# Row maxima stored by a transfer of single floats instead of through a transpose, and more places for visits of seven row maxima beside the mlp

## The chip, the cores and the metric

The kernel runs on one core of one Trainium2 chip, in one launch. The metric is the time of one execution on the device in microseconds (us). Five engines work side by side, each through its own list of instructions: PE (matrix products; PEld is its loading of the stationary operand), DVE (vector work and reductions), ACT (activations and copies), POOL (elementwise work, and it issues some transfers), and SP, which only issues transfers. They wait for one another through semaphores.

## What is computed

The reference, cut to what matters (S = 2048 tokens, D = 448, H = 16 heads of 28, F = 1792):

```python
g = sigmoid((x * gate_w).sum(-1, keepdims=True))
q, k, v = split_heads(x @ wqkv)                    # 16 heads of 28
scores = einsum("bhqd,bhkd->bhqk", q, k) * 28 ** -0.5
a = merge_heads(softmax(scores) @ v) @ wo
h = gelu(layernorm(x) @ w1 + b1)                   # 2048 x 1792
b = h @ w2 + b2
return g * a + (1 - g) * b
```

The softmax needs, for every head and every query, the largest score of its row. The kernel computes these row maxima in a pass of their own, ahead of the scores that are exponentiated.

## The kernel before, in words

**Stages.** Until 113 us PE computes q, k and v. From 113 us to 457 us the mlp runs in four column chunks `c` of 512 tokens: `mlp1` (L626: 14 tiles of 11 products each, into bank 0 or 7 by turns) and `mlp2` (L644: 4 tiles of 42 products each, also into banks 0 and 7 by turns). From 457 us to the end the attention runs over 16 chunks `n = 4 g + c`: four groups of four heads, four chunks of 512 queries.

PSUM is used as eight banks of 128 x 512 floats, `bank[:, 0]` to `bank[:, 7]`.

**Row maxima.** `RowMax` (L387) makes them for chunk after chunk. One chunk is 64 products of 28 x 512 (4 heads `j`, 4 query tiles `i`, 4 key pieces `k`; L450), each into a bank, each followed by a reduction of that bank along its row on DVE (L431; neighbouring banks in one instruction). The 64 columns of results are reduced to 16 (L461, tile `mf`, 128 x 16: a query's number within its tile is the partition). Then the chunk has to be closed (`close`, L410): PE transposes `mf` with the identity into a bank (L412), DVE multiplies the 16 x 128 result by -1 (L415, tile `mt`), and a transfer writes it to DRAM (L416, `ms`), where each head's 512 maxima lie in a row. The closing takes a place among the products as a 65th one: in the last bank of the first call of `issue` after the chunk's 64th product. 16 chunks are so 16 x 65 = 1040 places. `load_qm` (L556) later reads four rows of `ms` into the 29th row of each head in `qh`, so that the score product of 29 rows subtracts the maximum by itself. For the last chunk, that transfer is issued from step 12 of the 16 steps of the attention chunk before.

**Where the maxima stand on PE.** The order on PE is written out by the program. Beside the mlp, `Filler.run` is called after each product of the mlp (after some of `mlp2`'s), counts slots, and starts a *visit* when enough maxima are due: six products into banks 1 to 6, or seven, when the caller allows it (`seven(i)`, L622): then the bank of the neighbouring tile, 0 or 7, is used first. Seven are allowed after the products 4 to 7, counted from 0, of a tile of `mlp1` (not in the first column chunk) and for `f` from 1 to 11 in `mlp2`. Where only six are allowed, a visit waits until eight are due (`wait` = 2). `clear` keeps a visit from coming before DVE has reduced the one before it. `MLP_MAX` places (488) are spread over the mlp.

In the attention, PE alternates between the scores of five units (a unit: one head, 128 keys, 512 queries, three products, L577; U = 5) and the products of probabilities with v (L865). I call one such round a *slot*. A slot holds up to three maxima (`scores`, L567: one into bank 5 ahead, one into bank 6 in the middle, one into bank 5 at the end). The rest of the 1040 places is spread over 186 slots. When all of them are done, the slots become *late* ones: seven units in two halves, of four and three or of three and four (UL = 7), with the products with v between the halves, and no maxima.

**Queues.** Beside the mlp, SP issues the stores of the maxima (L416) and the loads of `qd` (L403), among the loads of the layernorm's input (L130) and the stores of the mlp's output (L663). In the attention `self.queue` is POOL: it issues the stores L416 and the loads L403 between its elementwise work and the transfers of `finish` (L783, L787, L789).

Of the kernel before, what the change touches and what calls it, by code (L numbers as in the profile page):

```python
# [30 lines left out]
MLP_MAX = 488  # L31
# [12 lines left out]
def kernel(ctx: ExitStack, tc: tile.TileContext, xt, wqk, wv, wo, xk, w1, b1, w2, b2,  # L44
# [17 lines left out]
    ms = [dram.tile([4, S], F32, name=f"ms{g}") for g in range(NG)]  # L62
# [324 lines left out]
    class RowMax:  # L387


        def __init__(self):  # L390
            self.queue = nc.sync
            self.qds = {}
            self.done = 0
            self.last = None
            self.load(0)
            self.begin(0)
# [13 lines left out]
        def close(self, ps):  # L410
            g, c = divmod(self.n - 1, NC)
            nc.tensor.transpose(ps[:4 * TPC, :P], self.last, ident)  # L412
            self.last = None
            mt = mpool.tile([4 * TPC, P], F32R, name="mt")
            nc.vector.tensor_scalar(mt, ps[:4 * TPC, :P], -1.0, None, op0=OP.mult)  # L415
            self.queue.dma_start(ms[g][:, c * CH:(c + 1) * CH].rearrange("j (i x) -> j i x", x=P), mt.bitcast(F32))  # L416

        def issue(self, banks, rows=None, close=65):

            held, closing = [], self.last is not None
# [11 lines left out]
            for b in banks:  # L434
                left = sum(len(x) for x in self.left)
                closes = closing and b == banks[-1] and left <= close
                if not (left or closes):
                    break
                self.done += 1
                if closes:  # L440
                    reduce()
                    self.close(bank[:, b])
                    continue
# [14 lines left out]
                if left == 1:  # L458
                    reduce()
                    self.last = mpool.tile([P, 4 * TPC], F32, name="mf")  # L460
                    nc.vector.reduce_max(self.last.rearrange("p (j i) -> p j i", j=4),  # L461
                                         self.mx.rearrange("p (k i j) -> p j i k", k=4, j=4), axis=AX)
                    if self.n + 1 < NG * NC:
# [103 lines left out]
    def scores(units, most, tiles, between=None, opening=None):  # L567
# [19 lines left out]
        if most > 0:  # L587
            filler.max.issue([5], [(units[0] + 3) % 4], close=56)
# [8 lines left out]
        for i in range(3):  # L597
            for p in last:
                product(p, i)
            if i == 0 and most > 1:  # L600
                filler.max.issue([6], [(units[0] + 1) % 4, (units[0] + 2) % 4], close=-1)
# [398 lines left out]
```

## Time and profile before

| | |
|---|---|
| median of 3 runs | 1100.08 us (1099.73 to 1100.36) |
| the profiled execution, its own time | 1099.34 us |
| its span, first to last instruction | 1097.5 us |
| PE busy | 1090.4 us (99% of the span) |
| DVE busy | 737.1 us (67%) |
| ACT busy | 638.1 us (58%) |
| POOL busy | 334.2 us (30%) |
| PE's granted clock, mean | 0.999 |
| products of row maxima (L450) | 1024 |
| transposes of row maxima (L412) | 16, 4.4 us in all |

How to read the rows that follow: a timeline row gives the start in us from the beginning of the span, the time from the first to the last instruction of the row, the engine, the line of the program, the operation, what it writes and reads, the shape, and how many instructions were merged into the row. Products overlap, so the distance from one start to the next says more than the length of a row. A group row gives count, busy time and the mean of one instruction in ns, then the idle time ahead of them and what ended it. Rows of waits name who waited for whom, with the total, the number of times and the longest. Rows of one line give the shortest, median and longest duration in ns. In the slots of the attention each product with v appears as two products in the timeline.

### The profile page before, as it was taken

The page shows a single profiled execution, that of the slowest core. Times are in us where ns is not written, and L with a number is a line of the kernel's source. Part 1 is how long each engine was busy: PE and PEld are TensorE (multiplying, and loading weights), DVE is VectorE, ACT ScalarE, POOL GpSimd, SP SyncE. Part 2 cuts the span into 40 slices and gives each one's busy share as a digit, 9 for nine tenths or more (in the row PEclk, how much of TensorE's full clock was granted, in tenths as well). Part 3 has the DMA queues.
Part 4 walks back from the last instruction along what each step waited for, and adds up shares of the span by engine and source line. Part 5 has one row for each costly group of instructions (what it writes and reads, how often), then busy time and mean ns, then how long its engine had stood idle before and what let it go on. Part 6 is the DMA issues. An engine that isn't in the chain of part 4 may idle for free.

```text
span 1097.5 us, 19765 instructions
## 1 busy us (share of the span) xinstructions
PE 1090.4 (99%) x8150; PEld 667.4 (61%) x8150; DVE 737.1 (67%) x958; ACT 638.1 (58%) x658; POOL 334.2 (30%) x357
## 2 busy tenths in 40 slices
PE   9999999999999999999999999999999999999998
PEld 7888877777778777744444444444444444464545
DVE  4553598988888988566766766666666767746103
ACT  5434651331240231478878878878878878848572
POOL 5015565243334340013202320321223024343260
PEclk9999999999999999999999999999999999999999
DMA  7988531011121032262000220012111003002011
GB/s 268 355 273 289 174 112 65 9 47 51 40 52 46 18 80 72 69 153 61 28 19 19 65 73 19 20 29 53 36 51 37 19 20 95 13 26 70 35 53 59
DMA packets 53078, 84.34 MB, mean 77 GB/s; under 512 B 8516, under 2 KB 28500, under 8 KB 52076
## 3 DMA queue, kind: packets, MB, share of 16 engines
q1 hardware_dynamic: 48732, 76.27, 22.4%
q0 software_dynamic: 4256, 6.81, 2.5%
q8 instruction: 64, 1.05, 0.4%
q14 instruction: 26, 0.21, 0.1%
HBM read 56.40 MB, written 26.49 MB: 76 GB/s over the span
## 4 chain that ended last, share of the span: by engine, by line
PE 96%; DVE 1%; issue 1%; ACT 1%; DMA 0%; SPq 0%; DVEq 0%; ACTq 0%
PE bank L865 22%; PE bank L577 20%; PE bank L450 15%; PE bank L634 12%; PE bank L221 5%; PE bank L650 4%; PE bank L656 4%; PE bank L651 4%; PE bank L233 3%; PE bank L323 2%; PE bank L762 1%; PE bank L763 1%; PE bank L764 1%; DVE mx L431 1%; DMA raw<-in_xt 0%
## 5 line engine op out<-in xcount | busy, mean ns | idle before, releaser
L431 DVE TENSOR_REDUCE mx<-bank 128x1 f32<-128x512 f32 (+2 forms) x735 | 635.1, 897 | 197.4 <-PE bank L450 184.3
L581 ACT ACTIVATE pt<-bank 128x1536 f32<-128x1536 f32 (+1 forms) x387 | 461.6, 1243 | 119.0 <-PE bank L577 119.0
L865 PE MATMUL bank<-pt,vg 128*32 128x512 f32 x1948 | 260.4, 602 | 0.1
L450 PE MATMUL bank<-khi,qd 28*128 28x512 f32 x512 | 241.3, 479 | 0.5
L450 PEld LDWEIGHTS bank<-khi,qd 28*128 28x128 f32 x512 | 92.3, 181 | 146.2 <-DVE mx L431 108.1
L577 PE MATMUL bank<-qh,klo 28*128 28x512 f32 x1024 | 172.3, 391 | 0.0
L577 PE MATMUL bank<-qh,khi 29*128 29x512 f32 x768 | 155.5, 480 | 0.8 <-ACT khi L581 0.5
L634 PE MATMUL bank<-y,w1f 128*128 128x512 f32 x616 | 152.0, 397 | 0.0
L634 PEld LDWEIGHTS bank<-y,w1f 128*128 128x128 f32 x616 | 112.6, 188 | 33.0 <-issue 11.1
L577 PE MATMUL bank<-ql,khi 28*128 28x512 f32 x768 | 128.8, 391 | 0.0
L642 POOL TENSOR_TENSOR hl<-h,hh 128x512 fp32r<-128x512 f32 x56 | 73.0, 1303 | 117.4 <-ACT hh L641 92.4
L783 POOL DMA_DIRECT2D lt<-ob x15 | 10.8, 723 | 273.0 <-DVE ob L782 248.7
L640 ACT ACTIVATE h<-bank,b1s 128x512 f32<-128x512 f32 x56 | 38.6, 689 | 94.8 <-PE bank L634 94.7
L865 PEld LDWEIGHTS bank<-pt,vg 128*32 128x32 f32 x1948 | 44.6, 108 | 77.3 <-issue 73.1
L577 PEld LDWEIGHTS bank<-qh,klo 28*128 28x128 f32 x1024 | 86.1, 185 | 3.4
L577 PEld LDWEIGHTS bank<-qh,khi 29*128 29x128 f32 x768 | 60.3, 182 | 39.7 <-ACT pt L581 24.3
L650 PE MATMUL bank<-w2h,hh 128*128 128x448 f32 x224 | 83.7, 374 | 0.0
L656 PE MATMUL bank<-w2h,hl 128*128 128x448 f32 x224 | 83.2, 372 | 0.0
L651 PE MATMUL bank<-w2l,hh 128*128 128x448 f32 x224 | 81.2, 363 | 0.0
L662 ACT ACTIVATE h<-bank 128x448 f32<-128x448 f32 x16 | 8.7, 546 | 123.0 <-PE bank L656 67.7
L450 PE MATMUL bank<-khr,qd 28*128 28x512 f32 x512 | 72.6, 460 | 0.2 <-DVE mx L431 0.2
L577 PEld LDWEIGHTS bank<-ql,khi 28*128 28x128 f32 x768 | 64.9, 185 | 11.9
(142 smaller groups left out, 1220.5 us busy)
## 6 DMA issues: line engine op xcount, KB each, us to landing
qk<-hl SPq DMA_DIRECT2D x28, 512.0 KB
raw<-in_xt SPq DMA_DIRECT2D x16, 256.0 KB
vs<-vt SPq DMA_DIRECT2D x16, 256.0 KB
s<-in_xt SPq DMA_DIRECT2D x16, 256.0 KB
rc<-rls POOLq DMA_DIRECT2D x60, 64.0 KB, 2.3
w1f<-in_xk SPq DMA_DIRECT2D x8, 448.0 KB
gbs<-h SPq DMA_DIRECT2D x16, 224.0 KB
klo<-qk SPq DMA_DIRECT2D x16, 224.0 KB
```

The lines of the kernel that those rows point to most:

```text
L221: nc.tensor.matmul(ps, a, b, start=(i == 0), stop=(i == len(ops) - 1))
L431: nc.vector.reduce_max(self.mx[:, at:at + n], bank[:, b:b + n] if n > 1 else bank[:, b], axis=AX)
L450: nc.tensor.matmul(bank[:, b], self.qds[self.n][r, i * P:(i + 1) * P], khi[self.n // NC][r, k * 512:(k + 1) * 512], start=True, stop=True)
L577: nc.tensor.matmul(bank[:, p], a[r, k * P:(k + 1) * P], b[r], start=(i == 0), stop=(i == 2))
L581: nc.scalar.activation(t, bank[:, at[0]:at[-1] + 1], AF.Exp, scale=SCALE)
L634: nc.tensor.matmul(ps, a, b, start=(i == 0), stop=(i == len(ops) - 1))
L640: nc.scalar.activation(h, ps, AF.Gelu_apprx_tanh, bias=b1s[:, f:f + 1])
L642: nc.gpsimd.tensor_sub(hl[f], h, hh[f].bitcast(F32))
L650: nc.tensor.matmul(a, hh[f][:, sl], w2h[f], start=(f == 0), stop=False)
L651: nc.tensor.matmul(a, hh[f][:, sl], w2l[f], start=False, stop=False)
L656: nc.tensor.matmul(a, hl[f][:, sl], w2h[f], start=False, stop=(f == NF - 1))
L865: nc.tensor.matmul(pv[32 * j:32 * j + 32, :], vg[n // NC][:, k, 32 * j:32 * j + 32], probs.pop(4 * step + j), start=(k == 0), stop=(k == N ...
```

## The change

- `close` goes, and with it the 16 transposes on PE, the 16 multiplications of 16 x 128 out of PSUM on DVE, and 16 places: a chunk has 64 places, all of them 1024.
- Instead, right behind the reduction to `last` (128 x 16), DVE multiplies that tile by -1 (`neg`), and a transfer writes it to DRAM as it lies: 128 partitions of 16 floats, each float to its own place, because neighbouring floats of a partition belong 128 floats apart. The transfer always stands in SP's queue, in the attention too. Each chunk has a tensor `ms` of its own.
- `MLP_MAX` is 475 instead of 488. In the attention the remaining places are spread at three per slot.
- Visits of seven are allowed after the products 3 to 8 of a tile of `mlp1` (before 4 to 7) and for `f` from 1 to 12 in `mlp2` (before 1 to 11).

```diff
-MLP_MAX = 488
+MLP_MAX = 475
...
-    ms = [dram.tile([4, S], F32, name=f"ms{g}") for g in range(NG)]
+    ms = [dram.tile([4, CH], F32, name=f"ms{n}") for n in range(NG * NC)]
...
-        def close(self, ps):
-            g, c = divmod(self.n - 1, NC)
-            nc.tensor.transpose(ps[:4 * TPC, :P], self.last, ident)
-            self.last = None
-            mt = mpool.tile([4 * TPC, P], F32R, name="mt")
-            nc.vector.tensor_scalar(mt, ps[:4 * TPC, :P], -1.0, None, op0=OP.mult)
-            self.queue.dma_start(ms[g][:, c * CH:(c + 1) * CH].rearrange("j (i x) -> j i x", x=P), mt.bitcast(F32))
...
                 if left == 1:
                     reduce()
-                    self.last = mpool.tile([P, 4 * TPC], F32, name="mf")
-                    nc.vector.reduce_max(self.last.rearrange("p (j i) -> p j i", j=4),
+                    last = mpool.tile([P, 4 * TPC], F32, name="mf")
+                    nc.vector.reduce_max(last.rearrange("p (j i) -> p j i", j=4),
                                          self.mx.rearrange("p (k i j) -> p j i k", k=4, j=4), axis=AX)
+                    neg = mpool.tile([P, P], F32R, name="mt")[:, :4 * TPC]
+                    nc.vector.tensor_scalar(neg, last, -1.0, None, op0=OP.mult)
+                    nc.sync.dma_start(ms[self.n].rearrange("j (i p) -> p (j i)", p=P), neg.bitcast(F32))
...
-        while filler.done < min(65 * NG * NC, 65 * (n + 1) + 9):
+        while filler.done < 64 * (n + 1):
             filler.max.issue([5])
         g, c = divmod(n, NC)
-        nc.sync.dma_start(qs[n][0][DH:P:32].bitcast(F32), ms[g][:, c * CH:(c + 1) * CH])
+        nc.sync.dma_start(qs[n][0][DH:P:32].bitcast(F32), ms[n])
...
-                filler.run(W1, seven(f) if 4 <= i < 8 else (), 2)
+                filler.run(W1, seven(f) if 3 <= i < 9 else (), 2)
...
-            more = seven(i) if 0 < f < NF - 2 else ()
+            more = seven(i) if 0 < f < NF - 1 else ()
...
-    filler.spread(nc.gpsimd, NG * NC * 65, ((NG * NC - 2) * NT + LQ - 1) * 4 // U - 2)
+    filler.spread(nc.gpsimd, NG * NC * 64, -(-(NG * NC * 64 - filler.done) // 3))
```

What this does to the order of the instructions, in numbers counted over the whole of PE's list:

| | before | changed |
|---|---|---|
| visits beside the mlp | 74 | 71 |
| of seven places / of six | 38 / 36 | 47 / 24 |
| products of maxima beside the mlp | 475 | 473 |
| transposes beside the mlp / in the attention | 7 / 9 | 0 / 0 |
| products of maxima in the attention | 549 | 551 |
| slots with maxima or a transpose | 187 | 184 |

Of the visits, `mlp1` has four fewer and `mlp2` one more. A line number of the changed kernel is lower by 10 to 15 behind the deleted function: its L435 is L450 of before, L565 is L577, L622 is L634, L853 is L865, L549 is L561, and the store stands at L450.

PE, second tile of `mlp1` in the second column chunk, before (`w1f_900` is this tile's weights, `y` the layernorm's output, `khr` and `qd` the two operands of the maxima; `w1f_927` belongs to the next tile):

```order
L634 MATMUL bank<-y_100,w1f_900 128x512
L634 MATMUL bank<-y_101,w1f_900 128x512
L634 MATMUL bank<-y_100,w1f_900 128x512 x2
L450 MATMUL bank<-khr,qd 128x512 x6
L634 MATMUL bank<-y_101,w1f_900 128x512
L634 MATMUL bank<-y_100,w1f_900 128x512 x2
L634 MATMUL bank<-y_101,w1f_900 128x512
L634 MATMUL bank<-y_100,w1f_900 128x512 x3
L634 MATMUL bank<-y_100,w1f_927 128x512
```

The same tile in the changed kernel (its weights are `w1f_912`, the next tile's `w1f_939`):

```order
L622 MATMUL bank<-y_112,w1f_912 128x512
L622 MATMUL bank<-y_113,w1f_912 128x512
L622 MATMUL bank<-y_112,w1f_912 128x512 x2
L622 MATMUL bank<-y_113,w1f_912 128x512
L622 MATMUL bank<-y_112,w1f_912 128x512 x2
L622 MATMUL bank<-y_113,w1f_912 128x512
L622 MATMUL bank<-y_112,w1f_912 128x512
L435 MATMUL bank<-khr,qd 128x512 x7
L622 MATMUL bank<-y_112,w1f_912 128x512 x2
L622 MATMUL bank<-y_112,w1f_939 128x512
```

The visit of six after product 3 has become a visit of seven after product 8; two products follow it, then the next tile begins in the bank that the visit used first.

PE, end of the last slot with maxima and what follows, before (`khi` and `klo` are the keys, `pt` probabilities):

```order
L450 MATMUL bank<-khi_3882,qd 128x512
L577 MATMUL bank<-qh,klo 128x512 x2
L577 MATMUL bank<-ql,khi_3882 128x512 x2
L865 MATMUL bank<-pt_9734,vg 32x512
L865 MATMUL bank<-pt_9757,vg 32x512 x3
L412 MATMUL bank<-ident,mf 16x128
L577 MATMUL bank<-qh,khi_3882 128x512 x3
L577 MATMUL bank<-qh,klo 128x512 x3
L577 MATMUL bank<-ql,khi_3882 128x512 x3
```

The same place in the changed kernel, three slots earlier in the program:

```order
L435 MATMUL bank<-khi_3890,qd 128x512
L565 MATMUL bank<-qh,klo 128x512 x2
L565 MATMUL bank<-ql,khi_3890 128x512 x2
L435 MATMUL bank<-khi_3890,qd 128x512
L853 MATMUL bank<-pt_9674,vg 32x512
L853 MATMUL bank<-pt_9684,vg 32x512 x2
L853 MATMUL bank<-pt_9709,vg 32x512 x3
L853 MATMUL bank<-pt_9719,vg 32x512 x2
L565 MATMUL bank<-qh,khi_3890 128x512 x4
```

The slot of five units that began with the transpose is gone; the first late group, four units and then three, follows at once.

SP, around the load of the last chunk's maxima (`qh<-ms`), before; the store that it reads stood in POOL's queue:

```order
L852 DMA vg<-gbs 128x4x448
L770 DMA out_y<-klo 128x448
L561 DMA qh<-ms_74 4x512
L770 DMA out_y<-klo 128x448 x3
L852 DMA klo<-gbs 128x4x448
```

And in the changed kernel, where the store (`ms_86<-mt`) stands in the same queue, directly ahead of the load:

```order
L840 DMA vg<-gbs 128x4x448
L450 DMA ms_86<-mt 128x16x1
L549 DMA qh<-ms_86 4x512
L758 DMA out_y<-klo 128x448 x4
L840 DMA klo<-gbs 128x4x448
```

More of the change, by code (lines that the diff above doesn't have):

```diff
@@ L435, in issue @@
                 left = sum(len(x) for x in self.left)
-                closes = closing and b == banks[-1] and left <= close
-                if not (left or closes):
+                if not left:
                     break
                 self.done += 1
[L440 to L443, printed above, removed]
                 most = max(range(4), key=lambda j: (len(self.left[j]), -j))
@@ L587, in scores @@
         if most > 0:
-            filler.max.issue([5], [(units[0] + 3) % 4], close=56)
+            filler.max.issue([5], [(units[0] + 3) % 4])
         if opening:
@@ L878 @@
         while u < 4 * steps:
-            if not late and filler.done >= NG * NC * 65:
+            if not late and filler.done >= NG * NC * 64:
                 late = [(mpool.tile([P, S], F32, name="khr", bufs=1) if g == MLP_G else
```

9 lines of the change are left out of this document (4 added, 5 removed).

## Prediction

> **What bounds the kernel now.** I read the page's busy times first, then the chain that ended last, then a table of busy times by stage: the mlp, and the attention while it has maxima.
>
> ```profile
> PE 1090.4 (99%) x8150; PEld 667.4 (61%) x8150; DVE 737.1 (67%) x958; ACT 638.1 (58%) x658; POOL 334.2 (30%) x357
> PE 96%; DVE 1%; issue 1%; ACT 1%; DMA 0%; SPq 0%; DVEq 0%; ACTq 0%
> 113.50:456.90 343.40, 343.19 (x1788) 261.02 (x1787) 290.65 (x218) 103.57 (x165) 128.84 (x100) 1.00 0.21 59
> 456.90:1015.00 558.10, 557.52 (x5269) 266.19 (x5268) 380.17 (x613) 441.43 (x374) 139.39 (x189) 1.00 0.18 47
> ```
>
> The reader is to see that PE holds the end in both stages: busy for 343.19 of 343.40 us, and 557.52 of 558.10 us (columns: PE, PEld, DVE, ACT, POOL). So what counts is how long PE's list is, in time between starts. DVE is the nearest rival beside the mlp: 290.65 of 343.40 us, 85%.
>
> **Visits beside the mlp.** The timeline of PE in `mlp1` has visits of six, of seven and one with a transpose:
>
> ```profile
> 211.44 0.73 PE L450 MATMUL bank<-khr,qd 28*128 28x512 f32 x6
> 212.11 3.24 PE L634 MATMUL bank<-y,w1f 128*128 128x512 f32 x13
> 215.28 0.74 PE L450 MATMUL bank<-khr,qd 28*128 28x512 f32 x6
> ...
> 219.12 0.74 PE L450 MATMUL bank<-khr,qd 28*128 28x512 f32 x7
> 219.78 4.17 PE L634 MATMUL bank<-y,w1f 128*128 128x512 f32 x17
> 223.88 0.73 PE L450 MATMUL bank<-khr,qd 28*128 28x512 f32 x5
> 224.54 0.28 PE L412 MATMUL bank<-ident,mf 128*16 128x128 f32 x1
> 224.58 0.71 PE L634 MATMUL bank<-y,w1f 128*128 128x512 f32 x2
> ```
>
> From visit to visit it is 3.84 us with 13 products of the mlp and 4.76 us with 17: 0.92 / 4 = 0.23 us for a product, and 3.84 - 13 x 0.23 = 0.85 us for a visit of six. The visit of seven costs the same: 4.76 - 17 x 0.23 = 0.85. Until the mlp goes on, a six takes 0.67 us (211.44 to 212.11) and a seven 0.66. Four heads lie in four row groups and run together, so the seventh product finds room. The price hangs on the visit, and a seven carries one maximum more for nothing. `mlp2` has the same price:
>
> ```profile
> 442.80 0.36 PE L651 MATMUL bank<-w2l,hh 128*128 128x448 f32 x1
> 443.09 0.73 PE L450 MATMUL bank<-khr,qd 28*128 28x512 f32 x7
> 443.76 0.47 PE L656 MATMUL bank<-w2h,hl 128*128 128x448 f32 x1
> 444.07 0.37 PE L650 MATMUL bank<-w2h,hh 128*128 128x448 f32 x1
> 444.27 0.36 PE L651 MATMUL bank<-w2l,hh 128*128 128x448 f32 x1
> ```
>
> 442.80 to 444.07 holds two steps of 0.20 (444.07 to 444.27) and the visit: 1.27 - 0.40 = 0.87. The order has 74 visits before and 71 now: **-3 x 0.85 = -2.55 us**. A visit that ends in a transpose lasts 0.70 us (223.88 to 224.58) against 0.67: seven such, **-0.2 us**.
>
> **Slots of the attention.** Starts of the first maximum of slots in a row (that of 661 us is left out), then a slot with a transpose, then late slots of three and four units:
>
> ```profile
> 652.42 0.50 PE L450 MATMUL bank<-khi,qd 28*128 28x512 f32 x1
> 655.98 0.49 PE L450 MATMUL bank<-khi,qd 28*128 28x512 f32 x1
> 658.67 0.50 PE L450 MATMUL bank<-khi,qd 28*128 28x512 f32 x1
> ...
> 664.08 0.50 PE L450 MATMUL bank<-khi,qd 28*128 28x512 f32 x1
> ```
>
> ```profile
> 562.29 0.50 PE L450 MATMUL bank<-khi,qd 28*128 28x512 f32 x1
> 563.88 0.28 PE L412 MATMUL bank<-ident,mf 128*16 128x128 f32 x1
> 565.08 0.49 PE L450 MATMUL bank<-khi,qd 28*128 28x512 f32 x1
> ...
> 1052.37 0.50 PE L577 MATMUL bank<-qh,khi 29*128 29x512 f32 x3
> 1054.28 0.51 PE L577 MATMUL bank<-qh,khi 29*128 29x512 f32 x4
> 1056.18 0.50 PE L577 MATMUL bank<-qh,khi 29*128 29x512 f32 x3
> ```
>
> A slot is 2.70 us, every fourth, with two steps of v, 3.56 us: four take 664.08 - 652.42 = 11.66 us for 20 units, 0.583 us a unit. A late pair takes 1056.18 - 1052.37 = 3.81 us for seven units, 0.544 us. Three slots fewer move 15 units from one price to the other: 15 x (0.544 - 0.583) = **-0.6 us**. The slot with a transpose in the place of a maximum takes 2.79 us against 2.70: the 128-row transpose stops the row groups from running together. There are eight of them (the ninth is one of the three slots counted). Each costs between 0.09, as here, and 0.28, the transpose's own length, if nothing runs beside it; I take 0.13, nearer to the slot that is measured: **-1.1 us**.
>
> **What the change puts in.** On DVE, L415 goes and a multiplication of 128 x 16 comes, in the same instruction list directly behind L461. Its nearest row is a reciprocal of the same shape; the two rows of the maxima's reductions stand below it:
>
> ```profile
> L785 DVE RECIPROCAL lt<-lt x15: 242/244/254, 500.0 to 1046.7; 128x16 f32<-128x16 f32 x15
> L431 DVE TENSOR_REDUCE mx<-bank x546: 675/691/694, 460.1 to 1011.8; 128x1 f32<-128x512 f32 x182
>   PE bank L450: 140.0, 177
> ```
>
> At 0.24 us as L785 it delays the next reduction, and by that bank 5 for the next slot, in nine slots: at most 9 x 0.24 = 2.2 us; nothing where DVE waits for PE, as it does ahead of 177 of the 546 reductions in the attention (140.0 us, last row). I take **+0.4 us**, nearer to nothing because most of DVE's slack lies there.
>
> A visit of seven after product 8 of `mlp1` leaves two products until the next tile writes the bank that the visit used first. In this row DVE begins 0.53 us after the visit of 203.24:
>
> ```profile
> 203.24 0.74 PE L450 MATMUL bank<-khr,qd 28*128 28x512 f32 x7
> 203.77 2.89 DVE L431 TENSOR_REDUCE mx<-bank 128x1 f32<-128x512 f32 x2 [0.38 <-PE bank L450]
> ```
>
> With 0.69 for the bank (L431 above) it is free 1.22 us after the visit's start; the next tile arrives after 0.67 + 0.31 + 0.23 = 1.21 us (0.31 is the first step behind a visit, 443.76 to 444.07). So about 0.1 us for a semaphore; the order has two such visits: **+0.2 us**, up to 1.4 if DVE is a whole reduction, 0.69, late in both.
>
> The store: 16 times 2048 floats that are not neighbours in DRAM.
>
> ```profile
> L416 SPq DMA_DIRECT2D ms<-mt x7: 599/612/668, 186.4 to 433.8; - x7
> DMA to landing us min/median/max: 1.7/1.8/2.6
> L542 SPq DMA_DIRECT2D vg<-vs x8: 386/446/1045, 413.0 to 795.2; - x8
> q1 hardware_dynamic: 48732, 76.27, 22.4%
> ```
>
> Issuing costs SP no more than before: `vg<-vs` has 4 or 12 x 128 separate rows, 512 or 1536 pieces, and takes 0.45 us, against 0.61 us for the store's 16 pieces. The landing isn't shown by any row. Below, 1.8 us as L416. Above, a packet for each float at SP's mean: 0.224 x 16 x 1097.5 / 48732 = 0.081 us; over 16 engines 128 x 0.081 = 10.3 us. What hides it: nobody reads `ms` soon but for the last chunk. Behind the store in SP's queue are loads that are wanted a chunk later and the mlp's stores; SP stands waiting for other engines between them anyway. Cost 0, with either landing. POOL loses nine stores from its queue and nobody waits for POOL here.
>
> The Trainium skill, "DMA: Bandwidth & Descriptors", "Rules for kernel authors", speaks against this change: a last dimension with a stride becomes one descriptor per element, and a plain transfer that transposes is called 19 times slower than the hardware's transpose. No run here shows a transfer of single floats; 19 x 1.8 would be an estimate of 34 us for one store.
>
> **Sum.** -2.55 - 0.2 - 0.6 - 1.1 + 0.4 + 0.2 = -3.85 us, taken as -3.8. The profiled execution's own 1099.34 us (span 1097.5) becomes 1095.5; it lies 0.7 under the median 1100.08, from which I count: **1096.3 us**. With the bounds: 0.28 for each of the eight and no new wait give -2.55 - 0.2 - 0.6 - 2.2 = -5.6, 1094.5 us; 0.09 each, 2.2 on DVE and 1.4 in the mlp give -2.55 - 0.2 - 0.6 - 0.7 + 2.2 + 1.4 = -0.4, 1099.7 us. This kernel's measurement tells about 0.2% (2.2 us) from no change, so between 1097.9 and 1102.3 counts as none.
>
> **Rival 1: DVE paces the mlp.** 473 maxima need DVE as long as 475 did. If PE, three visits shorter, only comes earlier to banks not yet reduced, the 2.55 us go into waits and 1.25 remain: 1098.8 us. For it: DVE's 85%. Against it, the waits of PE's loads for a reduction in the window from 180 to 456 us (total, times, longest):
>
> ```profile
> PEld bank L450 <- DVE mx L431: 0.6, 2, 0.3
> ```
>
> PE's loads waited for DVE twice in all that time. Chance 0.14.
>
> **Rival 2, slower: the last store lands late and holds the last chunk.** Its place is the load `qh<-ms` of chunk 15, directly behind the store on SP. Before:
>
> ```profile
> 1012.57 0.27 DVE L461 TENSOR_REDUCE mf<-mx 128x16 f32<-128x64 f32 x1
> 1036.64 0.50 PE L577 MATMUL bank<-qh,khi 29*128 29x512 f32 x4
> ```
>
> The last reduction ended at 1012.84; chunk 15 starts at 1036.64, 23.8 us later. Now the maxima end ten units earlier in the program (unit 925 and not 935 follows), at 0.544 another 5.4 us: 29.2 us. Multiplication 0.24, issue 0.6, load 0.5 + 1.8 leave 26 us for the landing. At 10.3 us nothing happens. If the floats go over four engines only, by the four rows of `ms`, 512 x 0.081 = 41.5 us, and PE stands for 15.5 us: 1096.3 + 15.5 = 1111.8 us. It decides from a landing of 26 us, 0.2 us a float over 16 engines; it is slower by over 0.2% from about 32 us. Against it: the store's source has 128 partitions. Chance 0.07.
>
> The skill's 34 us would cost 8 us here; its rule on how many engines a transfer uses ("How many engines (k)", under "Why a DMA increments its semaphore by 16 and not by 1", same page) takes the slowest dimension of both sides, 128 here, and so sixteen engines. By that rule there is no stall; no run here shows the spread.
>
> **Rival 3: more comes back.** In the attention POOL held the store L416 among its elementwise work. One wait on DVE may come from that:
>
> ```profile
> DVE lt L785 <- DMA lt<-ob: 5.4, 3, 4.2
> ```
>
> The transfers `lt<-ob` stand in the same queue of POOL; DVE waited 5.4 us for them in three places, with reductions behind it. Without that, up to 1.5 us more (I let a good quarter reach PE): 1094.8 us. Chance 0.06.
>
> That the change doesn't do what it says is excluded by the order: 71 visits, no transposes.
>
> **Chances.** My forecast 0.73, of which 0.66 is faster by over 0.2% and 0.07 within it; rival 1 0.14, of which 0.03 and 0.11; rival 2 0.07, slower by 0.06 with 0.01 within; rival 3 0.06, faster. Faster 0.75, within 0.2% 0.19, slower 0.06. The range 1094.5 to 1099.5 takes in the forecast's bounds but for the last 0.2 us, and rivals 1 and 3, and leaves out rival 2.
>
> **What would show it.** Right: no L412; 71 visits, still 0.85 us; the mlp's end near 454 us and not 457; slots at a chunk's end within 0.1 us of 2.70; stores landing within 26 us. Wrong: waits of PE's loads for L431 beside the mlp well over 0.6 us (rival 1), slots behind L449 over 2.9 us (the multiplication's term), PE idle ahead of chunk 15 (rival 2), or SP's `qd` or layernorm loads late enough to hold PE (none of my terms).

## The result and the profile after

The changed kernel takes **1148.56 us** (median of 5 runs, 1147.51 to 1151.35) against 1100.08 us before: ratio 1.0447, 95% interval 1.0431 to 1.0463. The prediction said 1096.3 us, and its range ended at 1099.5. The profiled execution has a span of 1146.8 us; that is 49.3 us more than 1097.5. The page after:

```profile
PE 1101.3 (96%) x8134; PEld 670.4 (58%) x8134; DVE 735.1 (64%) x967; ACT 637.7 (56%) x657; POOL 328.0 (29%) x348
...
PEclk9999999999999999979999998999999989999999
...
q1 hardware_dynamic: 81616, 76.34, 28.2%
...
PE 83%; issue 7%; DMA 6%; DVE 2%; POOL 1%; ACT 1%; SPq 0%; POOLq 0%; DVEq 0%; ACTq 0%
```

No engine got noticeably more work: PE's busy time is 10.9 us longer with 16 instructions fewer, that of DVE, ACT and POOL is no longer than before. PE holds 83% of the chain instead of 96%, and its granted clock dips in three slices (7, 8, 8). SP's queue moves 32884 packets more (48732 before) with hardly more bytes (76.34 MB against 76.27). Three starts in PE's timeline cut the program into stages: the mlp's first product, its last, and the first unit of the last group. Before, then after:

```profile
113.46 1.32 PE L634 MATMUL bank<-y,w1f 128*128 128x512 f32 x5
...
456.60 0.37 PE L656 MATMUL bank<-w2h,hl 128*128 128x448 f32 x1
...
903.09 0.39 PE L577 MATMUL bank<-qh,khi 29*128 29x512 f32 x1
```

```profile
114.11 1.09 PE L622 MATMUL bank<-y,w1f 128*128 128x512 f32 x4
...
455.29 0.37 PE L644 MATMUL bank<-w2h,hl 128*128 128x448 f32 x1
...
947.30 0.39 PE L565 MATMUL bank<-qh,khi 29*128 29x512 f32 x1
```

Ahead of the mlp 0.65 us more; the mlp 341.18 us instead of 343.14 (-2.0); the first three groups of the attention 492.0 instead of 446.5 (**+45.5**); from there to the end 199.5 instead of 194.4 (**+5.1**). Together 49.3 us.

The 45.5 us, by engine: DVE's waits for `lt<-ob`, PE's for a reduction, and the landing of the transfers `lt<-ob` (POOL issues them, once a chunk):

```profile
DVE lt L773 <- DMA lt<-ob: 35.5, 6, 10.8
...
PE bank L435 <- DVE mx L421: 30.4, 10, 9.8
```

```profile
L771 POOL DMA_DIRECT2D lt<-ob x15: 712/736/761, 496.0 to 1086.6; - x15
...
DMA to landing us min/median/max: 2.2/2.3/12.1
```

Before, DVE waited 5.4 us there, PE 0.2 us under that releaser, and the latest `lt<-ob` landed after 4.5 us. The first of the three long stalls, in the timelines of DVE, SP, POOL and PE (put in order of time):

```profile
494.61 0.27 DVE L446 TENSOR_REDUCE mf<-mx 128x16 f32<-128x64 f32 x1
494.91 0.17 DVE L449 TENSOR_SCALAR mt<-mf 128x16 fp32r<-128x16 f32 x1
495.11 0.39 SPq L450 DMA_DIRECT2D ms<-mt  x1
...
496.01 0.76 POOL L771 DMA_DIRECT2D lt<-ob  x1 [25.57 <-DVE mx L421]
...
497.19 2.02 DVE L421 TENSOR_REDUCE mx<-bank 128x1 f32<-128x512 f32 x3 [0.58 <-PE bank L435]
510.06 0.25 DVE L773 RECIPROCAL lt<-lt 128x16 f32<-128x16 f32 x1 [10.85 <-DMA lt<-ob]
...
510.92 0.79 PE L435 MATMUL bank<-khi,qd 28*128 28x512 f32 x1 [9.80 <-DVE mx L421]
```

SP issues the store of single floats at 495.11. POOL issues `lt<-ob`, 0.9 us later. DVE reaches the reciprocal that reads `lt` and stands 10.85 us, in order, with two reductions behind it; PE has no free bank for the next maximum and stands 9.80 us. The others begin at 702.7 and 910.3. A store comes every 21.3 slots (64 maxima, three a slot) and a chunk ends every 12.8 (64 units, five a slot), so every third store meets a chunk's end. A table of busy times with the granted clock (last columns: clock, DMA share, GB/s) shows PE in the stall:

```profile
480.00:495.00 15.00, 15.00 (x144) 7.06 (x140) 10.66 (x20) 12.43 (x11) 0.00 (x0) 1.00 0.05 13
...
499.00:515.50 16.50, 6.70 (x42) 2.15 (x42) 2.29 (x5) 3.46 (x4) 1.78 (x4) 0.64 0.69 89
```

Below, the *excess* is what the attention's 183 slots with maxima (185 before; the very first isn't counted) take above the prediction's two prices, 2.70 us, or 3.56 with two steps of v, and above the output projections that four of them hold: 3.2 us before, 49.4 after. The three slots with the long stalls are 12.3 + 11.3 + 9.8 = 33.4 of it.

The 5.1 us at the end: POOL's instruction DRAIN after its last work, ahead of the barrier in which all engines meet. Before, then after (shortest, median, longest in ns):

```profile
L995 POOLq DRAIN  x3: 40/102/1407, 1091.0 to 1097.3; - x3
```

```profile
L983 POOLq DRAIN  x3: 40/102/10557, 1135.4 to 1146.5; - x3
```

It lasts 10.56 us instead of 1.41, to 1145.99, and the program ends 0.8 us later. Not all of the longer DRAIN counts, because POOL was not the last at the barrier before. There its DRAIN was over at 1092.43, and SP, which waits for the stores of `out_y` to land, came to its own at 1096.7. After the change SP comes to it at 1141.1, and POOL's ends 4.9 us behind.

### The profile page after: what moved, and what is told of

Its sections match the earlier page's. It is cut to its first block, busy times and chain, and to the rows that moved or that the text cites. A ratio compares the mean times of both kernels' runs of the same rounds, so it can differ in the third digit from the quotient of the medians.

```text
span 1146.8 us, 19735 instructions
## 1 busy us (share of the span) xinstructions
PE 1101.3 (96%) x8134; PEld 670.4 (58%) x8134; DVE 735.1 (64%) x967; ACT 637.7 (56%) x657; POOL 328.0 (29%) x348
## 3 DMA queue, kind: packets, MB, share of 16 engines
q1 hardware_dynamic: 81616, 76.34, 28.2%
## 4 chain that ended last, share of the span: by engine, by line
PE 83%; issue 7%; DMA 6%; DVE 2%; POOL 1%; ACT 1%; SPq 0%; POOLq 0%; DVEq 0%; ACTq 0%
PE bank L853 17%; PE bank L565 15%; PE bank L622 13%; PE bank L435 13%; PE bank L221 5%; PE bank L638 4%; PE bank L644 4%; DMA lt<-ob 4%; PE bank L639 4%; PE bank L233 3%; PE bank L323 1%; PE bank L750 1%; DVE mx L421 1%; PE bank L751 1%; PE bank L752 1%
## 5 line engine op out<-in xcount | busy, mean ns | idle before, releaser
L569 ACT ACTIVATE pt<-bank 128x1536 f32<-128x1536 f32 x383 | 457.2, 1244 | 162.6 <-PE bank L565 159.2
L435 PE MATMUL bank<-khi,qd 28*128 28x512 f32 x512 | 244.4, 486 | 32.4 <-DVE mx L421 30.4
L853 PE MATMUL bank<-pt,vg 128*32 128x512 f32 x1930 | 266.3, 617 | 0.9 <-DVE ob L770 0.9
L435 PEld LDWEIGHTS bank<-khi,qd 28*128 28x128 f32 x512 | 94.1, 184 | 185.3 <-DVE mx L421 143.1
L565 PE MATMUL bank<-qh,klo 28*128 28x512 f32 x1024 | 174.9, 394 | 0.0
L565 PE MATMUL bank<-qh,khi 29*128 29x512 f32 x768 | 156.9, 483 | 0.7 <-ACT khr L569 0.3
L622 PE MATMUL bank<-y,w1f 128*128 128x512 f32 x616 | 151.3, 397 | 0.0
L622 PEld LDWEIGHTS bank<-y,w1f 128*128 128x128 f32 x616 | 112.8, 188 | 33.3 <-issue 10.5
L565 PE MATMUL bank<-ql,khi 28*128 28x512 f32 x768 | 130.5, 393 | 0.0
L853 PEld LDWEIGHTS bank<-pt,vg 128*32 128x32 f32 x1930 | 45.0, 110 | 82.4 <-issue 77.6
L565 PEld LDWEIGHTS bank<-qh,klo 28*128 28x128 f32 x1024 | 88.3, 187 | 3.6
L565 PEld LDWEIGHTS bank<-qh,khi 29*128 29x128 f32 x768 | 62.1, 184 | 41.9 <-ACT pt L569 24.7
L565 PEld LDWEIGHTS bank<-ql,khi 28*128 28x128 f32 x768 | 66.4, 187 | 12.1
L435 PE MATMUL bank<-khr,qd 28*128 28x512 f32 x512 | 72.0, 460 | 0.0
```

The lines of the kernel that those rows point to most:

```text
L435: nc.tensor.matmul(bank[:, b], self.qds[self.n][r, i * P:(i + 1) * P], khi[self.n // NC][r, k * 512:(k + 1) * 512], start=True, stop=True)
L565: nc.tensor.matmul(bank[:, p], a[r, k * P:(k + 1) * P], b[r], start=(i == 0), stop=(i == 2))
L569: nc.scalar.activation(t, bank[:, at[0]:at[-1] + 1], AF.Exp, scale=SCALE)
L622: nc.tensor.matmul(ps, a, b, start=(i == 0), stop=(i == len(ops) - 1))
L853: nc.tensor.matmul(pv[32 * j:32 * j + 32, :], vg[n // NC][:, k, 32 * j:32 * j + 32], probs.pop(4 * step + j), start=(k == 0), stop=(k == N ...
```

## The experiments

**Theory 1**: the single floats keep the 16 DMA engines busy, POOL's small transfer lands late behind them, and DVE's order turns that into a stall of PE. Rivals: the multiplication, the issue on SP, the new places. "Landing" is SP's wait for the last chunk's store, right behind its issue; "DVE" its waits for `lt<-ob`, sum and longest. (In the kernel before, POOL issues that store, and SP's wait holds POOL's delay too.) Times are medians; the other columns are of one profiled execution, which for held_store is the fastest of four (1110.78 to 1121.70 us) and for rows_of_16 the slowest of four (1106.45 to 1115.02).

| kernel | us | ratio, 95% interval | excess | DVE | landing | DRAIN |
|---|---|---|---|---|---|---|
| before | 1100.08 | | 3.2 | 5.4, 4.2 | 4.3 | 1.41 |
| after | 1148.56 | 1.0447 (1.0431 to 1.0463) | 49.4 | 35.5, 10.8 | 10.9 | 10.56 |
| held_store | 1112.89 | 1.0135 (1.0093 to 1.0177) | 12.2 | 5.4, 4.3 | 10.5 | 10.55 |
| late_reciprocal | 1145.03 | 1.0409 (1.0378 to 1.0439) | 17.8 | 2.7, 2.7 | 11.0 | 10.55 |
| late_in_012 | 1117.38 | 1.0175 (1.0149 to 1.0201) | 14.9 | 4.6, 4.2 | 10.7 | 10.55 |
| rows_of_16 | 1110.29 | 1.0084 (1.0059 to 1.0110) | 13.4 | 10.3, 4.3 | 1.2 | 10.56 |
| visits_alone | 1102.44 | 1.0024 (1.0014 to 1.0035) | 3.1 | 5.6, 4.0 | 6.4 | 1.74 |
| block_sp | 1106.80 | 1.0068 (1.0051 to 1.0084) | 5.9 | 5.7, 4.6 | 1.0 | 10.56 |
| block_pool | 1102.16 | 1.0019 (1.0010 to 1.0028) | 6.4 | 8.6, 4.4 | | 3.61 |
| block_mixed | 1099.34 | 0.9996 (0.9986 to 1.0005) | 4.6 | 5.0, 4.2 | 1.0 | 1.41 |
| store_on_sp | 1104.65 | 1.0042 (1.0027 to 1.0057) | 3.1 | 3.9, 3.9 | | 10.55 |
| quarter_store | 1137.44 | one run | 38.5 | 30.2, 10.0 | 8.5 | 10.55 |
| pitch_2 | 1126.01 | 1.0237 (1.0217 to 1.0258) | 26.4 | 23.0, 6.5 | 6.3 | 10.56 |
| pitch_16 | 1109.61 | 1.0088 (1.0068 to 1.0108) | 11.2 | 10.6, 4.3 | 3.8 | 10.56 |
| pitch_128 | 1110.66 | 1.0095 (1.0066 to 1.0125) | 12.1 | 7.7, 4.3 | 3.6 | 10.55 |
| blocks_512 | 1760.13 | 1.5999 (1.5768 to 1.6229) | 385.4 | 124.3, 55.3 | 61.7 | 10.55 |
| blocks_odd | 1155.65 | 1.0507 (1.0446 to 1.0568) | 57.7 | 38.0, 13.5 | 9.9 | 10.55 |

### The store away from the chunk's end (held_store)

```diff
+                if k == 8:
+                    filler.max.store()   # in the attention: multiplication and store, else at once
```

> The changed kernel, but in the attention the multiplication by -1 and the store of single floats are held back to step 8 of the attention chunk, half a chunk away from the transfer lt<-ob. Same 16 stores of 2048 floats, same places on PE. Theory 1 (only the meeting of store and lt<-ob costs): the three long stalls go, 1109 to 1117 us. Theory 2 (the store delays the loads behind it in SP's queue): about as slow as the changed kernel, 1140 to 1152 us. If every store costs PE some us whatever it meets, 1120 to 1140 us.

1112.89 us. The landing is as late as ever (10.5 us), but no `lt<-ob` stands behind it, and DVE waits no longer than before:

```profile
DVE lt L785 <- DMA lt<-ob: 5.4, 2, 4.3
SPq L561 <- DMA ms<-mt: 10.5, 1, 10.5
```

So it is the meeting of the store and `lt<-ob` that costs. What is left over the kernel before is DRAIN and an excess of 9 us: places of 1 to 2 us, 8 to 10 us behind a store.

### The reciprocal later, twice (late_reciprocal, late_in_012)

```diff
-STEPS = (2, 5, 7, 8, 9, 10)
+STEPS = (5, 7, 8, 9, 10, 11)
```

> The changed kernel with one line edited: in the attention, the reciprocal on DVE and the steps behind it come three slots later (STEPS 5, 7, 8, 9, 10, 11 instead of 2, 5, 7, 8, 9, 10). Theory 1: the store of single floats keeps the transfer lt<-ob, issued 0.6 to 0.9 us behind it, from landing for about 12 us; DVE stands in its reciprocal, reductions behind it, PE without banks. Then this edit lets DVE work on for 8 us more, the three stalls of 12.3, 11.3 and 9.8 us (33.4 us together) all but go, and the time is 1113 to 1119 us. Theory 2: the store, standing in SP's queue, delays the loads behind it and PE waits for those. Then nothing changes: 1146 to 1151 us.

1145.03 us, a miss by my own edit: in one chunk `finish` doesn't come to its last step, so one of the sixteen output tiles is neither projected (12 of 192 products) nor stored, and in the last group POOL's `oh` comes too late for the others. PE's timeline has it standing there for 5.80 us, and once more for 10.32 at 1056.33; the granted clock was 0.90 from 1010 to 1060 us:

```profile
990.17 0.74 PE L750 MATMUL bank<-woh,oh 128*128 128x448 f32 x1 [5.80 <-POOL oh L784]
```

```profile
1010.00:1060.00 50.00, 38.90 (x338) 18.65 (x340) 14.30 (x25) 26.75 (x21) 16.48 (x17) 0.90 0.14 39
```

The three long stalls of the first three groups were gone (excess 17.8). The second form moves the steps only where there are no projections:

```diff
-LSTEPS if late else STEPS
+LSTEPS if late else STEPS if n // NC == NG - 1 else (5, 8)
```

> The changed kernel with one edit: in the first three groups, whose finishes have no projections, VectorE's reciprocal comes up at the fifth slot after a chunk's end instead of the second, and POOL's products at the eighth instead of the fifth; the last group keeps its slots, and all is computed. Theory 1's second half (the late landing of lt<-ob costs time only because VectorE stands in order before the reciprocal and the reductions behind it don't run): lt<-ob lands as late as before, up to 12 us after its issue, but VectorE no longer stands for more than 3 us, the three long stalls go (the first two wholly, the third in chunk 10 too), the excess falls from 49 to 12 to 20 us, and with 4.9 us in POOL's last drain the time is 1108 to 1118 us. Rival (the transfers on which PE itself waits are late as well, so that the stalls stay under other names): 1135 us or more.

Met: 1117.38 us (1113.1 to 1122.6; the profiled execution is near the lower end, with a span of 1111.3). `lt<-ob` lands up to 12.7 us after its issue, later than in the changed kernel, and DVE no longer stands there (its one long wait, 4.2 us, is near the end, as in the kernel before, though at most 3 were expected). The landing of `lt<-ob`, then DVE's timeline, where the reciprocal comes at 509.38 without a wait:

```profile
DMA to landing us min/median/max: 2.2/2.3/12.7
```

```profile
507.95 1.51 DVE L421 TENSOR_REDUCE mx<-bank 128x1 f32<-128x512 f32 x2 [0.41 <-PE bank L435]
509.38 0.24 DVE L773 RECIPROCAL lt<-lt 128x16 f32<-128x16 f32 x1
```

So the lateness alone doesn't make the three stalls; the reciprocal's place in DVE's order does. An excess of 11.7 us over the kernel before is left.

### Rows out, single floats back in (rows_of_16)

```diff
-nc.sync.dma_start(ms[self.n].rearrange("j (i p) -> p (j i)", p=P), neg.bitcast(F32))
+nc.sync.dma_start(ms[self.n], neg.bitcast(F32))      # 128 rows of 64 bytes
...
+nc.sync.dma_start(qs[n][0][DH:P:32, i * P:(i + 1) * P].bitcast(F32),
+                  ms[n].rearrange("p (j i) -> j i p", i=TPC)[:, i])   # for i in range(TPC)
```

> The changed kernel, but the store writes rows: 128 rows of 16 floats as they lie, 64 bytes each, and the load of the maxima gathers single floats from DRAM, four loads of 4 x 128 floats for each chunk. So 128 pieces written instead of 2048, and 2048 pieces read instead of 4. Theory 1 (writing single floats to DRAM is what lasts, some 12 us for a store): no stall behind the stores, 1095 to 1100 us if single floats are read quickly. If 2048 pieces last as long in either direction, the stalls move to where the loads stand: 1105 to 1150 us.

1110.29 us; the landing of the store is 1.2 us. As many single floats are now read from DRAM as were written, and the three stalls don't come; slots of 3.6 us and twice about 2 us of excess are left. The time lies in the range for the case that single floats are as slow to read, but no stall like the three is seen. The rest is DRAIN and a start of the mlp 3.1 us later, which is no part of the edit (see the visits alone).

### Blocks of 32x32 in place of single floats (block_sp)

```diff
+nc.vector.transpose(m[:, 32:64].bitcast(F32), m[:, :32].bitcast(F32))   # behind the multiplication
+for b in range(4):
+    nc.sync.dma_start(ms[self.n].rearrange("j (i b x) -> b (j i) x", b=4, x=32)[b],
+                      m[32 * b:32 * b + 4 * TPC, 32:64].bitcast(F32))
```

> The changed kernel, whose maxima are turned by VectorE in blocks of 32x32 and stored on SP by four transfers of 16 rows of 32 floats (64 pieces of 128 bytes) instead of 2048 single floats; nothing else changes, and all is computed. Theory 1 (the 2048 pieces of four bytes hold the 16 DMA engines for about 10 us, and what POOL issues behind them, lt<-ob, lands late): the three stalls of 9.8 to 12.3 us go and so do the smaller ones of 2 to 3 us behind the other stores; the excess of the slots over their base price falls from 49.4 us to 3 to 8; POOL's last drain stays at 10.5 us (no stores on POOL), which leaves about 4.9 us at the end. Time 1099 to 1105 us. Rival (the issue on SP, the multiplication on VectorE at a chunk's end or the new places of the products make the stalls): 1140 us or more, with stalls still at every third store.

1106.80 us, 1.8 above the range, but its steps hold: no stalls (excess 5.9), DRAIN 10.56. (The mlp takes 342.9 us here, against 341.2 in the change.) Places, multiplication and SP's issue are those of the change, so none of the rivals makes the 45 us.

### How many floats, and how far apart (quarter_store, pitch_2, pitch_16, pitch_128)

```diff
+nc.sync.dma_start(ms[self.n].rearrange("j (i p) -> p j i", p=P)[:, 0], neg[:, :TPC].bitcast(F32))  # quarter_store
+nc.sync.dma_start(ms[self.n].rearrange("j (i p s) -> s p (j i)", p=P, s=16)[0], neg.bitcast(F32))  # s = 2, 16, 128
```

> The changed kernel, which stores the maxima of the first head of four only: 512 single floats instead of 2048. The other three rows of each chunk are filled 41 products earlier from an input (one transfer of three rows of 2 KB on SP), so that the softmax of three heads in four works with wrong maxima. Theory 1 in its form by rate (each of 16 engines writes its single floats one after another, 128 of them in about 10.9 us, 85 ns each): now 32 to an engine, 2.7 us; lt<-ob lands at most 3 us late, the three long stalls shrink to under 2 us each, and the time is 1104 to 1112 us (with 4.9 us of drain). Rival (a store of single floats lands about 10 us after its issue however many there are): three stalls of 8 to 12 us, 1138 us or more.

1137.44 us: theory 1 **in its form by rate fell**. A quarter of the floats lands in 8.5 us instead of 10.9, and the stalls stay.

```profile
DVE lt L774 <- DMA lt<-ob: 30.2, 6, 10.0
SPq L550 <- DMA ms<-mt: 8.5, 1, 8.5
```

So a new theory 3: floats written close together follow one another.

> The changed kernel, whose 2048 single floats of a chunk go to addresses 64 bytes apart instead of 4 (a region of 128 KB). What is read back as maxima are the first 2 KB of each row, filled 41 products earlier from an input by one more transfer, so that the softmax works with wrong maxima. Theory 3 (single floats written into the same 64 bytes follow one another, 16 of them, whether the store has 512 floats or 2048; this is what takes some 10 us): every float has 64 bytes of its own now, the store lands in about 3 us, the three long stalls go, the excess of the slots over their base price falls from 49 to under 12 us, and the time is 1102 to 1112 us. Theory 1 (so many pieces to an engine, each so long): 2048 pieces as before, three stalls of 8 to 12 us, 1138 us or more. Theory 4 (any store of single floats takes about 10 us to land): the same, 1138 us or more.

> As the kernel with 64 bytes from float to float, but with 8 bytes from one to the next, so that 8 floats share 64 bytes instead of 16. Theory 3: the landing and with it the three long stalls are about half as long, 3 to 6 us each, excess 20 to 32 us, time 1118 to 1132 us. Theories 1 and 4: stalls of 8 to 12 us, 1138 us or more.

Both as theory 3 said: 1109.61 and 1126.01 us. The same 2048 floats land in 3.8 us at 64 bytes from one to the next, and in 6.3 us at 8. Of the kernel with 64 bytes, then 8:

```profile
DVE lt L774 <- DMA lt<-ob: 10.6, 5, 4.3
SPq L550 <- DMA ms<-mt: 3.8, 1, 3.8
```

```profile
DVE lt L774 <- DMA lt<-ob: 23.0, 5, 6.5
SPq L550 <- DMA ms<-mt: 6.3, 1, 6.3
```

> As the kernel with 64 bytes from float to float, but with 512 bytes, so that no two floats share 512 bytes (region 1 MB). If the piece that neighbours share is 64 bytes: nothing more is gained, the last store lands in 3.5 to 4.1 us and the time is 1108 to 1111 us. If it is 512 bytes (8 floats share one at 64 bytes from float to float): a little more, landing 3.0 to 3.4 us, waits for lt<-ob below 2 us, time 1105 to 1108 us. Against both: the time rises, because the wide region costs something of its own.

1110.66 us, landing 3.6: nothing more is gained beyond 64 bytes, which speaks against 512 bytes as the piece that neighbours share; a gain of some tenths couldn't have been told. That it is 64 bytes isn't shown: 8 bytes from float to float still cost something and 64 no longer do, and nothing between was tried.

### Neighbours, or a small stretch of DRAM (blocks_512, blocks_odd)

```diff
+nc.sync.dma_start(ms[self.n].rearrange("j (i s p) -> s p (j i)", p=P, s=16)[0], neg.bitcast(F32))  # blocks_odd: s=17
```

> The changed kernel, whose 16 blocks of 128 floats (one for each head and tile of 128 rows) lie 8 KB apart, while the floats in a block stay neighbours, 4 bytes apart; the region is 128 KB, as in the kernel with 64 bytes from float to float. What is read back as maxima comes from an input for the most part, as there. Theory 3 (neighbours in 64 or 512 bytes follow one another): stalls as in the changed kernel, DVE's waits for lt<-ob 8 to 11 us in three places, the last store landing in 9 to 11 us, 1138 us or more. Rival (the small stretch of DRAM that all writes go to): as with 64 bytes from float to float, landing 3.5 to 4.5 us, 1107 to 1113 us.

1760.13 us: **neither theory had that.** Neighbours as in the change, in 16 blocks 8 KB apart, and the landing is 61.7 us:

```profile
DVE lt L774 <- DMA lt<-ob: 124.3, 6, 55.3
SPq L550 <- DMA ms<-mt: 61.7, 1, 61.7
```

> As the kernel with 16 blocks of 128 neighbouring floats 8 KB apart, but with 8.5 KB (8704 bytes) from block to block, so that the blocks don't share the lower bits of their addresses. If neighbours in 64 or 512 bytes follow one another whatever the distance of the blocks: landing and stalls as in the changed kernel, last store 9 to 12 us, 1138 to 1160 us. If only places far apart that share lower bits of the address count (blocks at 8 KB fall on one, neighbours cost nothing): last store 3.5 to 5 us, 1106 to 1115 us. If distance has nothing to do with the bits: as with 8 KB, 50 us or more and above 1600 us.

```profile
DVE lt L774 <- DMA lt<-ob: 38.0, 5, 13.5
SPq L550 <- DMA ms<-mt: 9.9, 1, 9.9
```

1155.65 us, landing 9.9: at 8.5 KB the neighbours cost what they cost in the change, over a stretch of 136 KB. So closeness costs by itself, and 8 KB from block to block of neighbours is a second price on top. The 8 KB alone are not: in pitch_16 the floats of one partition for neighbouring tiles of 128 rows lie 128 x 64 bytes = 8 KB apart too, and that store lands in 3.8 us. Which bits of the address make it wasn't tried.

### POOL's DRAIN (store_on_sp, block_pool, block_mixed)

```diff
-            self.queue.dma_start(ms[g][:, c * CH   # the kernel before: store_on_sp
+            nc.sync.dma_start(ms[g][:, c * CH
...
-                        nc.sync.dma_start(   # block_sp: block_pool
+                        self.queue.dma_start(
...
+nc.vector.reduce_max(..., negate=True)   # block_mixed: no multiplication; b == 3 on self.queue, else SP
```

> The kernel before, with one edit: its nine stores of transposed maxima (16 rows of 512 bytes) that POOL issued in the attention are issued by SP. Theory on the end: POOL's last drain goes from 1.4 to 10.5 us, and the time rises by 4 to 5.5 us, to 1104 to 1105.5; no stall behind a store, since its pieces are of 512 bytes. Rival: the drain stays at 1.4 us (it is owed to the single floats), and the time is 1099 to 1101 us.

> As the kernel with 32x32 blocks, but its four transfers are issued by the queue that issued the stores before the change (POOL in the attention). Theory on the end (POOL's last drain takes 10.5 us where its nine stores have gone to SP, and 1.4 to 1.7 us where they are there): the drain is back at 1.4 to 1.8 us, and the time is 4 to 5 us below that of the same blocks on SP: 1095 to 1100 us, near or a little below the kernel before. Rival (the drain has to do with the rest of the change, as the places of the products or the end of the program): drain 10.5 us and the same time as the blocks on SP, within 1.5 us.

> The kernel with 32x32 blocks, with two edits: the sign is turned in the reduction itself, so that the multiplication goes, and of a chunk's four transfers three are issued by SP and one by the queue of the stores before the change, so that POOL issues 131 transfers as in the kernel before (122 in the changed kernel, 158 with all four on POOL). Theory on the end (POOL's last drain is 10.5 us at 122 transfers, 1.4 at 131, 1.7 at 135 and 3.6 at 158, about 0.08 us more with each): the drain is 1.4 to 1.5 us again, 2.2 us below the kernel with all four on POOL. Time 1098 to 1101 us, the kernel before within its uncertainty. Rival (the drain goes by what is stored by whom, not by the count): 3 us or more of drain, 1102 us or more.

The first is met: nine stores of ordinary rows moved from POOL to SP, and nothing else, make DRAIN 10.55 us and the program 4.6 us longer. block_pool is 4.6 us below block_sp, as expected, but its DRAIN is 3.61 us and not 1.4 to 1.8, and its time 2 us above the range. DRAIN isn't what the 2 us are: it was over at 1097.8, and SP came to its own only at 1099.6. Against block_mixed, which has no multiplication and issues fewer transfers on POOL, block_pool takes 1.2 us more in the mlp and 1.8 more of excess. The length of DRAIN goes with the count of POOL's transfers, not with whose stores they are: block_mixed, with the count of the kernel before, has its DRAIN to the nanosecond, and visits_alone, with four more loads of `qd` on POOL and no store more, has 1.74 us. Of store_on_sp, block_pool and block_mixed:

```profile
L995 POOLq DRAIN  x3: 40/102/10554, 1091.1 to 1102.2; - x3
```

```profile
L989 POOLq DRAIN  x3: 40/102/3611, 1094.2 to 1100.1; - x3
```

```profile
L988 POOLq DRAIN  x3: 40/102/1407, 1091.5 to 1097.8; - x3
```

block_mixed is the change without its two costs, and with 16 transposes of 32x32 blocks on DVE in place of the multiplications: 1099.34 us (1098.8 to 1101.3), 10 us below any version with single floats, and the same as the kernel before within the interval.

### The visits alone (visits_alone)

```diff
-                filler.run(W1, seven(f) if 4 <= i < 8 else (), 2)
+                filler.run(W1, seven(f) if 3 <= i < 9 else (), 2)
...
-            more = seven(i) if 0 < f < NF - 2 else ()
+            more = seven(i) if 0 < f < NF - 1 else ()
```

> The kernel before with the other half of the change alone: seven maxima allowed after products 3 to 8 of a tile and for f from 1 to 12; transposes, closings and 488 places as before. Theory A (a visit costs 0.85 us whether of six or seven): some two or three visits fewer, 1097.5 to 1099 us. Theory B (DVE paces the mlp, or the tighter places make tiles wait): 1100 us or more.

1102.44 us, slower and not faster, the time of theory B. But the mlp itself is 1.3 us shorter with two visits fewer, as theory A has it; it starts 1.5 us later, and the part behind it takes about 2 us more: five products of maxima have moved to the attention, where the maxima end in 187 slots instead of 185. The start lies in no edit: it shifts in the first 14 us, where all these kernels are alike, by -0.3 to 3.1 us from kernel to kernel. What sets it stays open.

## Why the prediction was wrong, point by point

- **The step that failed**: "Cost 0, with either landing", because "nobody reads `ms` soon but for the last chunk". The landing was about right (10.9 us, after 10.3), and nobody did read `ms`. But the working asked only who reads the store and what SP has behind it. The transfers behind it in the 16 DMA engines are POOL's too, and `lt<-ob`, 0.9 us later, has DVE in order behind it. The count of slots (21.3 and 12.8) told that every third store would meet one. 45.5 us instead of 0.
- The 10.3 us were right by chance. They rest on 128 floats to an engine at 0.081 us; with 32 to an engine it is still 8.5 us, and with 128 at 64 bytes' distance 3.8. What counts is how the floats lie in DRAM.
- "POOL loses nine stores from its queue and nobody waits for POOL here": at the end everybody does. DRAIN, +4.9 us in the span of store_on_sp (1102.4 against 1097.5), is most of the rest of the result. No row of before showed that it depends on what POOL issued.
- **The mlp**: -2.55 us forecast (-2.55 - 0.2 + 0.2), -2.0 measured; the price of a visit held within 0.04 us (sevens in `mlp1` are that much dearer than before). Waits of PE's loads for a reduction there rose from 0.6 us to 2.1 (rival 1 in small), which may be the difference:

```profile
PEld bank L435 <- DVE mx L421: 2.1, 7, 0.4
```

- **The slots**: -1.1 for the transposes and +0.4 for the multiplication gave an excess of 3.2 - 1.1 + 0.4 = 2.5 us. Without stalls it is 5.9 (block_sp, which has a DVE transpose besides) and 4.6 without the multiplication (block_mixed): a fall of 0.7 was forecast, and it is a rise of 1.4 to 2.7. The transposes were about right: the eight slots that hold one took 1.2 us above their price before. What was mis-sized is the chunk's end, put at +0.4 and at most 2.2: the slots in which the reduction to `mf` stands took 0.7 us above their price in all before and take 3.4 after (the first, from 493.26 to 496.66, takes 3.40 us, over the 2.9 that the prediction named as a sign against it). The multiplication's own length, 0.17 us in the row DVE L449 above and not 0.24, is too short for that (9 x 0.17 = 1.5); why the chunks' ends cost more isn't settled.
- **Rival 2** had the late landing and put it at the wrong reader: the last chunk had its 26 us, and 10.9 was no matter there. From unit 768 on, little but DRAIN is lost (5.1 us, of which 4.9).
- **Rival 3** quoted the very row, DVE's waits for `lt<-ob`, and read it as a gain, since only POOL's queue was thought of. It went from 5.4 to 35.5 us.
- Two places of the Trainium skill bear on this. "DMA: Bandwidth & Descriptors", "Rules for kernel authors", warns of a strided last dimension; the estimate of 34 us from its factor of 19 had the direction right and was far above the 10.9 us that the runs show. (The factor is one against the hardware's transpose, which no run here has; the 1.8 us that it was put on are the landing of an ordinary store.) "Issuing engines are not separate DMA queues", same page of the skill, says that transfers of SP and POOL run on the same 16 engines and interleave; the stall at 495 us agrees, and the prediction didn't ask it.
- Around 10 us of excess lie behind other stores: held_store and late_in_012, without the long stalls, still have 9 and 12 over the kernel before. That too seems to go with the floats' closeness: without the slots where DVE waits longest for `lt<-ob`, pitch_16 has 6.5 us (11.2 - 4.7) and pitch_128 5.0 (12.1 - 4.0 - 3.1), as little as block_sp. What is waited for there stays open.

So with both costs taken away the change is worth nothing that can be measured (0.9986 to 1.0005): block_mixed gains 1.5 us in the mlp and three slots, and loses 1.4 us of excess, at the chunks' ends, and 1.0 us by a later start.

## What to carry to other kernels

A transfer that nobody waits for is not free: list what any queue issues in the 10 us behind it, and which engine stands in order before that. For a transpose on the way to DRAM, count the separate small writes that lie close together (8 bytes apart still cost here, 64 no longer); a 32x32 transpose on DVE with rows of 128 bytes (landing 1.0 us) takes that away. When transfers move to or from POOL, look at its last DRAIN, and at what the other engines wait for at the end: only what goes beyond that counts.

## What the runs showed of the hardware that was not expected

- 2048 writes of 4 bytes land in 10.9 us where they are neighbours, 6.3 at 8 bytes, 3.8 at 64, 3.6 at 512; 512 neighbours in 8.5; and 16 blocks of 128 neighbours in 61.7 us at 8192 bytes from block to block, 9.9 at 8704. Single floats without neighbours don't suffer from the 8192 bytes (pitch_16, 3.8).
- POOL's DRAIN by the transfers that POOL had issued: 10.55 us at 122, 1.41 at 131, 1.74 at 135, 3.61 at 158. From 131 on it is 0.082 us for each ((3.61 - 1.41) / 27); between 122 and 131 it falls by 9 us, and why wasn't tried. It costs only what lasts beyond SP's wait for the last stores: 4.9 us of the 10.55, nothing of the 3.61.
- A wait of PE of 8 to 10 us costs some 2.4 us more than itself: the slots of the three stalls lost 12.3, 11.3 and 9.8 us for waits of 9.80, 8.76 and 7.51. Behind the first, PE worked at a granted clock of 0.50 up to 515.5 us, then 0.66 up to 518, and at the full clock from there on:

```profile
511.00:515.50 4.50, 4.50 (x21) 1.09 (x25) 1.15 (x2) 0.00 (x0) 1.40 (x4) 0.50 0.51 138
515.50:518.00 2.50, 2.50 (x22) 1.68 (x22) 1.37 (x3) 1.03 (x1) 0.79 (x2) 0.66 1.04 309
518.00:530.00 12.00, 12.00 (x120) 5.50 (x112) 8.37 (x14) 9.72 (x9) 5.18 (x7) 1.00 0.18 56
```
